# Gate of the first expert layer: first maximum worked in the PSUM bank of the logits, running sums left to TensorE, ranks issued three parts sooner

## The chip, the cores and the metric

One core of a Trainium2 chip runs the whole program. The metric is device time in microseconds (us), the median of the runs of a kernel. TensorE is written PE here, its weight loads PEld, VectorE DVE, ScalarE ACT, GpSimd POOL, SyncE SP.

## The reference

An attention with squared ReLU scores gives 9984 rows of 256 numbers. Two expert layers follow, each with 8 experts and one expert per row: a gate picks the expert by the first maximum of 8 logits, and the softmax weight of that maximum scales the expert's output.

```
x  = attention(u, v, z).reshape(9984, 256)
# first expert layer, for rows with x @ w_skip > 0, the others pass
e  = argmax(x @ w_gate);  p = softmax(x @ w_gate)[e]
x  = x + p * (relu(x @ w1[e]) @ w2[e])
# second expert layer, all rows
l  = x @ w_gate2 + modality_bias[modality_id]
e  = argmax(l);  p = softmax(l)[e]
out = p * (relu(x @ w1'[e]) @ w2'[e])
```

## The kernel before

The attention comes first; it sorts its rows by expert into a list in DRAM (`rows1`). The first expert layer (class `Moe1`) then walks that list in tiles of 348 rows (`P1` x `G1` = 116 x 3), one expert per tile, and the second layer (`Moe2`) walks `rows2` in tiles of 512. Everything is in the order in which the code is written: each engine runs its own instructions in that order, and waits where an operand is not ready or a buffer not free.

A tile is one call of `Moe.turn`. It has sixteen parts. In the parts h0 to h7 `hidden(f)` makes 128 of the 1024 hidden columns: six matmuls into a PSUM buffer `ph` (there are three), then a ReLU copy `hh` on ACT (L795) and the remainder `hl` on DVE (L796). In o0 to o7 `out_part(f)` multiplies `hh` and `hl` by the second weight, six matmuls again (L894). Between parts stand hooks, listed in `Moe1.PLAN`. The hook `("after",)` advances by one step the generator `Moe1.after`, which finishes the tile before: it forms that tile's logits for the second gate, picks the expert, ranks the rows within each expert, and sends them to `rows2`. So the gate of one tile is worked between the matmuls of the next.

Of its eleven steps these matter here, with the part behind which each stands: `logits` (h4) transposes the logits to rows on PE into a buffer `m` (pool `ps_m`, two buffers of one PSUM bank each, taken in turn) and DVE adds the bias (L939, tile `mlg`); `first` (h5) is `FirstMax`, five DVE instructions that mark the first maximum of three times 8 logits; `sums` (h6) masks the marks (L959, tile `ohbb`) and adds them up over the three groups (L963, `cumb`); `exp` (h7) is the exponential on ACT (L124); `rows(0)` (o0) and `rows(2)` (o1) transpose the output on PE into two more buffers `m` (L926) and write `x_out` on DVE (L930); `ranks` (o2) counts by three matmuls into a buffer `m` (L969 to L971) and makes the target indices on DVE (L974 to L980, L727). After the tile `send` scatters `x_out` to `rows2` from POOL, which also splits the second weight (L678) during h2 to o0.

There are 16 calls of `after`. Fifteen follow this order (`gate_first`). The last, under the first tile of the second layer, does the rows first, and its tile takes both buffers `m` for its own output (`take_y`) right behind `first` and `exp`.

Of the kernel before, what the change touches and what calls it, by code (L numbers as in the profile page):

```python
# [10 lines left out]
F32 = mybir.dt.float32  # L11
F32R = mybir.dt.float32r
BF16 = mybir.dt.bfloat16
I32 = mybir.dt.int32
AF = mybir.ActivationFunctionType
ALU = mybir.AluOpType
AX = mybir.AxisListType
# [6 lines left out]
E, F = 8, 1024  # L24
# [80 lines left out]
class FirstMax:  # L105


    def __init__(self, nc, pool, k, lg, P, n, tag):
        self.nc = nc
        sh = [P, n, E]  # L110
        t = lambda name, *sh: pool.tile([128, *sh], F32, name=name + tag)[:P]
        mx, self.df, self.hot = t("mx", n), t("df", n, E), t("hot", n, E)
        self.ex, self.sm = t("ex", n, E), t("sm", n)
        df, hot = self.df, self.hot
        nc.vector.tensor_reduce(mx, lg, axis=AX.X, op=ALU.max)
        nc.vector.tensor_tensor(df, lg, mx.unsqueeze(2).to_broadcast(sh), op=ALU.subtract)
        nc.vector.scalar_tensor_tensor(
            hot, df, 0.0, k.desc[:P].unsqueeze(1).to_broadcast(sh), op0=ALU.is_equal, op1=ALU.mult
        )
        nc.vector.tensor_reduce(mx, hot, axis=AX.X, op=ALU.max)  # L120
        nc.vector.tensor_tensor(hot, hot, mx.unsqueeze(2).to_broadcast(sh), op=ALU.is_equal)
# [622 lines left out]
class Moe:  # L744
# [74 lines left out]
    def turn(self, follow, after, hooks=None):  # L819

        nc, sh = self.nc, self.sh
        nxt = []

        def hook(what, *args):
            if what == "next":
                nxt.extend(follow())
                nxt[0].load_rows(nxt[2])
                sh.load(0, nxt[1])
            elif what == "after":
                next(after, None)  # L830
            elif what == "w2":
                sh.split(1, args[0], nc.gpsimd)
            elif what == "w1":
                sh.split(0, args[0], nc.vector)
            elif what == "x":
                nxt[0].x_transposed(args[0])
            elif what == "load w2":
                sh.load(1, nxt[1])
            else:
                what()  # L840

        plan = self.PLAN if hooks is None else hooks
        for h in plan["start"]:
            hook(*h)
        self.work({at: [lambda h=h: hook(*h) for h in hs] for at, hs in plan.items()})
        for _ in after:
            pass


class Moe1(Moe):  # L850
# [45 lines left out]
    def after(self, lim, current, ps=None, gate_first=True):  # L896

        nc, k, P, G, T = self.nc, self.k, self.P, self.G, self.T
        s, sh = self.p, self.sh
        y = s.tile([128, 2, T], F32, name="yS")  # L900
        yh = s.tile([128, 2, T], F32R, name="yh")
        yl = s.tile([128, 2, T], F32R, name="yl")
        x, xo, lt = self.x_cur, self.x_out[:P], self.lt
        lg = s.tile([128, G, E], F32, name="mlg")[:P]
        gate = {}

        def taken():
            for d in range(2):
                nc.scalar.copy(y[:, d], self.y[d])
                nc.scalar.copy(yh[:, d], self.y[d])  # L910

        def low(d):
            nc.vector.tensor_tensor(yl[:, d], y[:, d], yh[:, d].bitcast(F32), op=ALU.subtract)

        def logits_t():
            lt_ps = sh.ps_m.tile([2 * E, T], F32, name="m")
            for i, (d, m) in enumerate(((0, yh), (1, yh), (0, yl), (1, yl))):
                nc.tensor.matmul(lt_ps, self.wg[:, d], m[:, d], start=(i == 0), stop=(i == 3))
            nc.scalar.copy(lt[:2 * E], lt_ps)

        def rows(g0):
            y_ps = sh.ps_m.tile([128, 2, D], F32, name="m")[:P]
            gs = range(g0, min(g0 + 2, G))
            for g in gs:
                for d in range(2):
                    nc.tensor.transpose(  # L926
                        y_ps[:, g - g0, d * 128:(d + 1) * 128], y[:, d, g * P:(g + 1) * P], k.ident
                    )
            for g in gs:
                nc.vector.scalar_tensor_tensor(  # L930
                    xo[:, g, 0:D], y_ps[:, g - g0], x[:, g, C_G1:C_G1 + 1], x[:, g, 0:D], op0=ALU.mult, op1=ALU.add
                )

        def logits():
            lg_ps = sh.ps_m.tile([128, G, E], F32, name="m")[:P]
            for g in range(G):
                nc.tensor.matmul(lg_ps[:, g], lt[:, g * P:(g + 1) * P], k.pairs, start=True, stop=True)
            for g in range(G):
                nc.vector.scalar_tensor_tensor(  # L939
                    lg[:, g], lg_ps[:, g], x[:, g, C_G1:C_G1 + 1], x[:, g, C_B2:C_B2 + E],  # L940
                    op0=ALU.mult, op1=ALU.add,
                )

        def masks():
            gate["drop"] = s.tile([128, G], F32, name="mk_drop")[:P]
            nc.vector.memset(gate["drop"], 0.0)
            nc.vector.tensor_copy(sh.lim, lim.rearrange("p t o -> p (t o)"))
            mk = gate["mk"] = self.counted(sh.lim)[:, 0]
            nc.vector.tensor_scalar(gate["drop"], mk, -BIG, BIG, op0=ALU.mult, op1=ALU.add)
            gate["cum"] = s.tile([128, G + 1, E], BF16, name="cumb")[:P]  # L950
            nc.vector.memset(gate["cum"][:, 0], 0.0)

        def first():
            gate["first"] = FirstMax(nc, s, k, lg, P, G, "b")

        def sums():
            ohb, cum = s.tile([128, G, E], BF16, name="ohbb")[:P], gate["cum"]
            gate["ohb"] = ohb
            nc.vector.tensor_tensor(  # L959
                ohb, gate["first"].hot, gate["mk"].unsqueeze(2).to_broadcast([P, G, E]), op=ALU.mult  # L960
            )
            for g in range(G):
                nc.vector.tensor_tensor(cum[:, g + 1], cum[:, g], ohb[:, g], op=ALU.add)  # L963

        def ranks():
            w, ohb, cum = G * E, gate["ohb"], gate["cum"]
            flat = lambda t: t.rearrange("p n e -> p (n e)")
            rk_ps = (ps or sh.ps_m).tile([128, w + E], F32, name="m")
            nc.tensor.matmul(rk_ps[:P, 0:w], k.tri[:P, :P], flat(ohb), start=True, stop=False)  # L969
            nc.tensor.matmul(rk_ps[:P, 0:w], k.ones[:P, :P], flat(cum[:, 0:G]), start=False, stop=True)  # L970
            nc.tensor.matmul(rk_ps[:, w:], k.ones[:P], cum[:, G], start=True, stop=True)  # L971
            rk = s.tile([128, G, E], F32, name="rkb")[:P]
            carry = self.carry
            nc.vector.tensor_tensor(  # L974
                rk, rk_ps[:P, 0:w].rearrange("p (n e) -> p n e", n=G), carry[:P].to_broadcast([P, G, E]), op=ALU.add
            )
            nc.vector.tensor_tensor(carry[:, 0], carry[:, 0], rk_ps[:, w:], op=ALU.add)
            nc.vector.tensor_tensor(rk, rk, ohb, op=ALU.mult)
            at = s.tile([128, G], F32, name="atb")[:P]
            nc.vector.tensor_reduce(at, rk, axis=AX.X, op=ALU.add)  # L980
            self.sc.index(at, gate["drop"])

        def close():
            nc.vector.tensor_copy(xo[:, :, C_TID], x[:, :, C_TID])
            nc.vector.reciprocal(xo[:, :, C_G2], gate["first"].total())
            if current is not None:
                self.load_rows(current(), self.x_cur)

        both = lambda *f: lambda: [i() for i in f]
        exp = lambda: gate["first"].exp()  # L990
        begin = [both(masks, taken), lambda: low(0), lambda: low(1), logits_t]
        if gate_first:
            steps = begin + [logits, first, sums, exp, lambda: rows(0), both(lambda: rows(2), close), ranks]
        else:
            steps = begin + [lambda: rows(0), lambda: rows(2), logits, both(first, exp), both(close, sums), ranks]
        for step in steps[:-1]:
            step()
            yield
        steps[-1]()
# [319 lines left out]
```

## Time and profile before

| | before |
|---|---|
| median of 3 runs | 1509.66 us (1508.88 to 1510.91) |
| profiled execution | 1509.91 us |
| its span, first to last instruction | 1507.8 us |
| PE busy | 1471.7 us, 98% |
| DVE busy | 1082.8 us, 72% |
| ACT busy | 949.7 us, 63% |
| POOL busy | 614.7 us, 41% |

The span is what the trace covers; 2.1 us of the profiled execution lie around it. A busy PE means that matmuls follow one another; the duration of one in a row is longer than its distance to the next, since they overlap, so the distance of starts is what a matmul costs.

### The profile page before, as it was taken

The numbers are of one execution on the slowest core, as the hardware profiler recorded it, in microseconds if no ns is written. First come the engines' busy times: TensorE is split into PE (matmuls) and PEld (weight loads), VectorE is DVE, ScalarE is ACT, GpSimd is POOL, SyncE is SP. The second block draws the span as 40 slices with busy tenths as digits, with TensorE's granted clock in tenths as the row PEclk, the third lists the DMA queues.
The fourth block names the chain that finished last, engine by engine and source line by source line (L and its number), as shares of the span: only waits on it lengthen the run. The fifth ranks groups of instructions, "written<-read, shape, count | busy, mean of one in ns | idle before, by whom it ended". The sixth has DMA issues, their size and how long they took to land. (4 is left out here: it accounts for less than half of the span.)

```text
span 1507.8 us, 35395 instructions
## 1 busy us (share of the span) xinstructions
PE 1471.7 (98%) x11020; PEld 1268.7 (84%) x11020; DVE 1082.8 (72%) x2587; ACT 949.7 (63%) x1713; POOL 614.7 (41%) x865
## 2 busy tenths in 40 slices
PE   7999999999999999999999999999999999999998
PEld 5888888888887888888799999998888888888886
DVE  7788887888878888778787777777655555455553
ACT  7777777778777777776555555555445445455453
POOL 3022222223333233332365656655455354354454
PEclk9999999999999999999999999999999999999999
DMA  9011211112111141002145555554344433433440
GB/s 370 23 44 64 71 37 42 43 57 72 38 43 44 57 144 35 29 16 89 54 137 165 182 178 174 170 168 154 133 148 144 143 125 130 155 131 126 143 147 27
DMA packets 50212, 160.28 MB, mean 106 GB/s; under 512 B 13797, under 2 KB 15707, under 8 KB 40896
## 3 DMA queue, kind: packets, MB, share of 16 engines
q1 hardware_dynamic: 29232, 124.24, 25.1%
q0 software_dynamic: 20736, 34.71, 6.5%
q8 instruction: 61, 1.00, 0.3%
q14 instruction: 39, 0.32, 0.1%
q10 hardware_dynamic: 144, 0.02, 0.0%
HBM read 124.24 MB, written 46.55 MB: 113 GB/s over the span
## 5 line engine op out<-in xcount | busy, mean ns | idle before, releaser
L700 POOL DMA_INDIRECT rows<-r,ix x160 | 205.5, 1285 | 339.0 <-DVE xs L347 244.5
L334 PE MATMUL o<-ah,vh 64*128 64x512 f32 (+1 forms) x1560 | 311.4, 386 | 9.2 <-DVE xs L347 9.2
L334 PE MATMUL o<-al,vh 64*128 64x512 f32 (+1 forms) x1560 | 303.0, 384 | 0.0
L334 PE MATMUL o<-ah,vl 64*128 64x512 f32 (+1 forms) x1560 | 301.7, 383 | 0.0
L796 DVE SCALAR_TENSOR_TENSOR hl<-ph,hh 128x512 fp32r<-128x512 f32 (+1 forms) x288 | 176.5, 614 | 156.7 <-ACT hh L795 156.0
L678 POOL TENSOR_TENSOR w<-w2raw,w 128x256 fp32r<-128x256 f32 x282 | 198.8, 744 | 171.5 <-issue 154.8
L291 ACT ACTIVATE t<-s 128x1024 f32<-128x1024 f32 (+2 forms) x201 | 201.0, 1001 | 87.2 <-PE s L288 80.7
L305 DVE TENSOR_TENSOR al<-t,ah 128x1024 fp32r<-128x1024 f32 (+2 forms) x201 | 240.0, 1194 | 18.3 <-PE m L371 0.5
L795 ACT ACTIVATE hh<-ph 128x512 fp32r<-128x512 f32 (+1 forms) x288 | 155.8, 541 | 115.1 <-PE ph L793 102.9
L303 ACT ACTIVATE t<-t 128x1024 f32<-128x1024 f32 (+2 forms) x201 | 208.1, 1036 | 5.9
L793 PE MATMUL ph<-mxh,zA 128*128 128x512 f32 (+1 forms) x576 | 209.7, 364 | 2.1 <-PEq L1315 1.4
L304 DVE CAST ah<-t 128x1024 fp32r<-128x1024 f32 (+2 forms) x201 | 136.3, 678 | 103.1 <-ACT t L303 100.5
L793 PE MATMUL ph<-mxh,zB 128*128 128x512 f32 (+1 forms) x576 | 206.9, 359 | 1.0 <-issue 1.0
L793 PE MATMUL ph<-mxl,zA 128*128 128x512 f32 (+1 forms) x576 | 207.1, 360 | 0.3 <-DVE mxl L783 0.3
L334 PEld LDWEIGHTS o<-ah,vh 64*128 64x128 f32 x1560 | 150.5, 185 | 45.4 <-DVE xs L347 16.7
L334 PEld LDWEIGHTS o<-al,vh 64*128 64x128 f32 x1560 | 150.4, 185 | 27.3
L334 PEld LDWEIGHTS o<-ah,vl 64*128 64x128 f32 x1560 | 146.8, 185 | 27.4
L782 ACT CAST mxh<-m 128x512 fp32r<-128x512 f32 (+1 forms) x72 | 37.8, 526 | 167.2 <-PE m L778 163.3
L894 PE MATMUL o<-hh,w 128*128 128x348 f32 x512 | 129.5, 336 | 0.0
L793 PEld LDWEIGHTS ph<-mxh,zA 128*128 128x128 f32 x576 | 108.4, 188 | 19.6 <-issue 3.7
L288 PE MATMUL s<-zA,zB 64*128 64x512 f32 (+1 forms) x400 | 124.5, 389 | 0.0
L288 PE MATMUL s<-zB,zA 64*128 64x512 f32 (+1 forms) x400 | 122.1, 389 | 0.0
(236 smaller groups left out, 3050.8 us busy)
## 6 DMA issues: line engine op xcount, KB each, us to landing
w1raw<-in_w SPq DMA_DIRECT2D x36, 1024.0 KB, 6.8
w2raw<-in_w SPq DMA_DIRECT2D x36, 1024.0 KB, 5.1
x_in<-rows SPq DMA_DIRECT2D x20, 520.0 KB, 3.4
vraw<-in_v SPq DMA_DIRECT2D x20, 512.0 KB, 5.0
ut<-in_uT SPq DMA_DIRECT2D x20, 512.0 KB, 4.2
x_cur<-rows SPq DMA_DIRECT2D x16, 351.8 KB, 3.1
x_in<-rows SPq DMA_DIRECT2D x15, 351.8 KB, 3.2
rows<-x_in POOLq DMA_DIRECT2D x8, 536.0 KB, 12.0
```

The lines of the kernel that those rows point to most:

```text
L288: nc.tensor.matmul(s[:, i, :n], w[p, k], x[p, q], start=(j == 0), stop=(j == 2))
L291: nc.scalar.activation(t[:, i, :n], s[:, i, :n], AF.Relu, scale=SCALE)
L303: nc.scalar.activation(t[:, i, :n], t[:, i, :n], AF.Square)
L304: nc.vector.tensor_copy(h[:, i, :n], t[:, i, :n])
L305: nc.vector.tensor_tensor(l[:, i, :n], t[:, i, :n], h[:, i, :n].bitcast(F32), op=ALU.subtract)
L334: nc.tensor.matmul(o[half][d][:, :n], w[p, d * 128:d * 128 + 128], x[p, :n], start=(u == 0 and j == at[0]), stop=(u == 9 and j == at[-1]),)
L678: lo_engine.tensor_tensor(l[:, c], src[:, c], h[:, c].bitcast(F32), op=ALU.subtract)
L700: i = tc.nc.gpsimd.indirect_dma_start(out=out, out_offset=bass.IndirectOffsetOnAxis(ap=ix, axis=0), in_=rows, in_offset=None, bounds_check ...
L793: nc.tensor.matmul(ps, w, x, start=(i == 0), stop=(i == len(mms) - 1))
L795: nc.scalar.activation(h, ps, AF.Relu)
L796: nc.vector.scalar_tensor_tensor(l, ps, 0.0, h.bitcast(F32), op0=ALU.max, op1=ALU.subtract)
L894: nc.tensor.matmul(self.y[d], w[:, dd], h[f], start=(f == 0 and i == 0), stop=(f == 7 and i == 2))
```

## The change

`FirstMax` may now be given the tiles for the difference and the marks. In `Moe1.after` the buffer `m` of the logits is four times as wide: the transposed logits, the logits with bias, the difference and the marks are four pieces of one PSUM bank. The masking stands in `first`; the step `sums` and its running sums are gone, and `ranks` adds with matmuls by ones instead, six matmuls in place of three. `exp` is now behind h6, `ranks` behind h7, and the last DVE instruction of the old `ranks` stays behind o2 as `place`.

```diff
@@ -105,11 +105,12 @@
 class FirstMax:
 
 
-    def __init__(self, nc, pool, k, lg, P, n, tag):
+    def __init__(self, nc, pool, k, lg, P, n, tag, df=None, hot=None):
         self.nc = nc
         sh = [P, n, E]
         t = lambda name, *sh: pool.tile([128, *sh], F32, name=name + tag)[:P]
-        mx, self.df, self.hot = t("mx", n), t("df", n, E), t("hot", n, E)
+        mx = t("mx", n)
+        self.df, self.hot = (t("df", n, E), t("hot", n, E)) if df is None else (df, hot)
         self.ex, self.sm = t("ex", n, E), t("sm", n)
         df, hot = self.df, self.hot
         nc.vector.tensor_reduce(mx, lg, axis=AX.X, op=ALU.max)
@@ -901,7 +902,6 @@
         yh = s.tile([128, 2, T], F32R, name="yh")
         yl = s.tile([128, 2, T], F32R, name="yl")
         x, xo, lt = self.x_cur, self.x_out[:P], self.lt
-        lg = s.tile([128, G, E], F32, name="mlg")[:P]
         gate = {}
 
         def taken():
@@ -932,7 +932,8 @@
                 )
 
         def logits():
-            lg_ps = sh.ps_m.tile([128, G, E], F32, name="m")[:P]
+            gate["ps"] = sh.ps_m.tile([128, 4, G, E], F32, name="m")[:P]
+            lg_ps, lg = gate["ps"][:, 0], gate["ps"][:, 1]
             for g in range(G):
                 nc.tensor.matmul(lg_ps[:, g], lt[:, g * P:(g + 1) * P], k.pairs, start=True, stop=True)
             for g in range(G):
@@ -947,28 +948,26 @@
             nc.vector.tensor_copy(sh.lim, lim.rearrange("p t o -> p (t o)"))
             mk = gate["mk"] = self.counted(sh.lim)[:, 0]
             nc.vector.tensor_scalar(gate["drop"], mk, -BIG, BIG, op0=ALU.mult, op1=ALU.add)
-            gate["cum"] = s.tile([128, G + 1, E], BF16, name="cumb")[:P]
-            nc.vector.memset(gate["cum"][:, 0], 0.0)
 
         def first():
-            gate["first"] = FirstMax(nc, s, k, lg, P, G, "b")
-
-        def sums():
-            ohb, cum = s.tile([128, G, E], BF16, name="ohbb")[:P], gate["cum"]
-            gate["ohb"] = ohb
+            ps = gate["ps"]
+            gate["first"] = FirstMax(nc, s, k, ps[:, 1], P, G, "b", ps[:, 2], ps[:, 3])
+            gate["ohb"] = s.tile([128, G, E], BF16, name="ohbb")[:P]
             nc.vector.tensor_tensor(
-                ohb, gate["first"].hot, gate["mk"].unsqueeze(2).to_broadcast([P, G, E]), op=ALU.mult
+                gate["ohb"], gate["first"].hot, gate["mk"].unsqueeze(2).to_broadcast([P, G, E]), op=ALU.mult
             )
-            for g in range(G):
-                nc.vector.tensor_tensor(cum[:, g + 1], cum[:, g], ohb[:, g], op=ALU.add)
 
         def ranks():
-            w, ohb, cum = G * E, gate["ohb"], gate["cum"]
+            w, ohb = G * E, gate["ohb"]
             flat = lambda t: t.rearrange("p n e -> p (n e)")
             rk_ps = (ps or sh.ps_m).tile([128, w + E], F32, name="m")
             nc.tensor.matmul(rk_ps[:P, 0:w], k.tri[:P, :P], flat(ohb), start=True, stop=False)
-            nc.tensor.matmul(rk_ps[:P, 0:w], k.ones[:P, :P], flat(cum[:, 0:G]), start=False, stop=True)
-            nc.tensor.matmul(rk_ps[:, w:], k.ones[:P], cum[:, G], start=True, stop=True)
+            for g in range(1, G):
+                nc.tensor.matmul(
+                    rk_ps[:P, g * E:w], k.ones[:P, :P], flat(ohb[:, 0:G - g]), start=False, stop=(g == G - 1)
+                )
+            for g in range(G):
+                nc.tensor.matmul(rk_ps[:, w:], k.ones[:P], ohb[:, g], start=(g == 0), stop=(g == G - 1))
             rk = s.tile([128, G, E], F32, name="rkb")[:P]
             carry = self.carry
             nc.vector.tensor_tensor(
@@ -976,9 +975,11 @@
             )
             nc.vector.tensor_tensor(carry[:, 0], carry[:, 0], rk_ps[:, w:], op=ALU.add)
             nc.vector.tensor_tensor(rk, rk, ohb, op=ALU.mult)
-            at = s.tile([128, G], F32, name="atb")[:P]
-            nc.vector.tensor_reduce(at, rk, axis=AX.X, op=ALU.add)
-            self.sc.index(at, gate["drop"])
+            gate["at"] = s.tile([128, G], F32, name="atb")[:P]
+            nc.vector.tensor_reduce(gate["at"], rk, axis=AX.X, op=ALU.add)
+
+        def place():
+            self.sc.index(gate["at"], gate["drop"])
 
         def close():
             nc.vector.tensor_copy(xo[:, :, C_TID], x[:, :, C_TID])
@@ -990,9 +991,9 @@
         exp = lambda: gate["first"].exp()
         begin = [both(masks, taken), lambda: low(0), lambda: low(1), logits_t]
         if gate_first:
-            steps = begin + [logits, first, sums, exp, lambda: rows(0), both(lambda: rows(2), close), ranks]
+            steps = begin + [logits, first, exp, ranks, lambda: rows(0), both(lambda: rows(2), close), place]
         else:
-            steps = begin + [lambda: rows(0), lambda: rows(2), logits, both(first, exp), both(close, sums), ranks]
+            steps = begin + [lambda: rows(0), lambda: rows(2), logits, both(first, exp), close, both(ranks, place)]
         for step in steps[:-1]:
             step()
             yield
```

In the built program this moves the following rows. The names are the program's: `ph`, `hh`, `hl`, `o` and `m` as above, `w` the second weight, `tri` and `ones` constants. First PE, in a tile of the first layer outside the loop (the loop's tile has the same rows with register instructions between). Before, the end of h7 and o0:

```order
L793 MATMUL ph<-mxh,zA_113 128x348
L793 MATMUL ph<-mxl,zA_113 128x348
L793 MATMUL ph<-mxh,zB_114 128x348
L894 MATMUL o_11060<-hh_11037,w_11033 128x348 x2
L894 MATMUL o_11060<-hl_11045,w_11033 128x348
L894 MATMUL o_11061<-hh_11037,w_11033 128x348 x2
L894 MATMUL o_11061<-hl_11045,w_11033 128x348
L926 MATMUL m<-ident,yS 116x128 x4
```

And now the same place:

```order
L794 MATMUL ph<-mxl,zA_113 128x348
L794 MATMUL ph<-mxh,zB_114 128x348
L964 LDWEIGHTS tri
L964 MATMUL m<-ohbb,tri 116x24
L966 LDWEIGHTS ones
L966 MATMUL m<-ohbb,ones 116x16
L966 LDWEIGHTS ones
L966 MATMUL m<-ohbb,ones 116x8
L970 LDWEIGHTS ones
L970 MATMUL m<-ohbb,ones 128x8
L970 LDWEIGHTS ones
L970 MATMUL m<-ohbb,ones 128x8
```

A third such pair and then o0 (L895) follow. The matmuls on the masked marks `ohbb` stood behind o2 as three, and now stand between h7 and o0 as six.

DVE in the last tile of the first layer, from the logits on. Before:

```order
L939 SCALAR_TENSOR_TENSOR mlg<-m,x_cur 116x8 x3
L796 SCALAR_TENSOR_TENSOR hl_11050<-ph,hh_11042 128x348
L115 TENSOR_REDUCE mxb<-mlg 116x3
L116 TENSOR_TENSOR dfb<-mlg,mxb 116x24
L117 SCALAR_TENSOR_TENSOR hotb<-dfb,desc 116x24
L120 TENSOR_REDUCE mxb<-hotb 116x3
L121 TENSOR_TENSOR hotb<-hotb,mxb 116x24
L796 SCALAR_TENSOR_TENSOR hl_11051<-ph,hh_11043 128x348
L959 TENSOR_TENSOR ohbb<-hotb,mk 116x24
L963 TENSOR_TENSOR cumb<-cumb,ohbb 116x8 x3
L796 SCALAR_TENSOR_TENSOR hl_11052<-ph,hh_11044 128x348
```

And now:

```order
L940 SCALAR_TENSOR_TENSOR m<-m,x_cur 116x8 x3
L797 SCALAR_TENSOR_TENSOR hl_11050<-ph,hh_11042 128x348
L116 TENSOR_REDUCE mxb<-m 116x3
L117 TENSOR_TENSOR m<-m,mxb 116x24
L118 SCALAR_TENSOR_TENSOR m<-m,desc 116x24
L121 TENSOR_REDUCE mxb<-m 116x3
L122 TENSOR_TENSOR m<-m,mxb 116x24
L956 TENSOR_TENSOR ohbb<-m,mk 116x24
L797 SCALAR_TENSOR_TENSOR hl_11051<-ph,hh_11043 128x348
L797 SCALAR_TENSOR_TENSOR hl_11052<-ph,hh_11044 128x348
L973 TENSOR_TENSOR rkb<-m,carry 116x24
L976 TENSOR_TENSOR carry<-carry,m 128x8
```

The masking stands one `hl` sooner, the running sums are gone, the additions on the ranks follow the last `hl`, and the logits, difference and marks lie in `m`.

PE in the last call of `after`, under the first tile of the second layer, with what each row waits for (the number behind an engine's name only marks its semaphore). Before, o0 begins:

```order
L1056 MATMUL o_11060<-w_11033,hh_11037 128x512 [waits Pool_49]
L1059 MATMUL o_11060<-w_11033,hl_11045 128x256
L1056 MATMUL o_11061<-w_11033,hh_11037 128x512
L1059 MATMUL o_11061<-w_11033,hl_11045 128x256
L1056 MATMUL m<-w_11033,hh_11037 128x512 [waits DVE_49]
L1059 MATMUL m<-w_11033,hl_11045 128x256
L1056 MATMUL m<-w_11033,hh_11037 128x512 [waits DVE_49]
```

And now:

```order
L1057 MATMUL o_11060<-w_11033,hh_11037 128x512 [waits Pool_49]
L1060 MATMUL o_11060<-w_11033,hl_11045 128x256
L1057 MATMUL o_11061<-w_11033,hh_11037 128x512
L1060 MATMUL o_11061<-w_11033,hl_11045 128x256
L1057 MATMUL m<-w_11033,hh_11037 128x512 [waits DVE_49]
L1060 MATMUL m<-w_11033,hl_11045 128x256
L1057 MATMUL m<-w_11033,hh_11037 128x512 [waits Activation_49]
```

The order is the same; the second matmul into a buffer `m`, the one that held the logits, waits for ACT in place of DVE.

## Rows read from the trace of the kernel before

**Rows 1.** One loop tile: stretch, length, PE, PEld, DVE, ACT, POOL busy, PEclk, DMA, GB/s.

```profile
925.92:943.87 17.95, 17.95 (x122) 17.58 (x122) 14.14 (x47) 10.65 (x25) 11.19 (x18) 1.00 0.55 178
```

**Rows 2.** Waits of PE, 759 to 1063 us (waiter, releaser, us, times, longest).

```profile
PE m L969 <- DVE x_out L930: 3.8, 4, 1.6
```

**Rows 3.** Timeline of that tile, DVE: the chain behind h5 (start, us, instruction).

```profile
933.79 0.52 DVE L796 SCALAR_TENSOR_TENSOR hl<-ph,hh 128x348 fp32r<-128x348 f32 x1 [0.72 <-ACT hh L795]
934.23 0.17 DVE L115 TENSOR_REDUCE mxb<-mlg 116x3 f32<-116x24 f32 x1
...
934.64 0.63 DVE L117 SCALAR_TENSOR_TENSOR hotb<-dfb,desc 116x24 f32<-116x24 f32 x1
...
935.52 0.45 DVE L121 TENSOR_TENSOR hotb<-hotb,mxb 116x24 f32<-116x24 f32 x1
...
936.33 0.17 DVE L959 TENSOR_TENSOR ohbb<-hotb,mk 116x24 bf16<-116x24 f32 x1
```

**Rows 4.** Timeline of that tile, PE: o0, row transposes, ranks.

```profile
934.78 0.48 PE L894 MATMUL o<-hh,w 128*128 128x348 f32 x2
...
935.74 0.60 PE L926 MATMUL m<-ident,yS 128*116 128x128 f32 x4
...
937.45 0.38 PE L926 MATMUL m<-ident,yS 128*116 128x128 f32 x2
...
938.61 0.18 PE L969 MATMUL m<-ohbb,tri 116*116 116x24 bf16 x1
938.64 0.20 PE L970 MATMUL m<-cumb,ones 116*116 116x24 bf16 x1
938.69 0.17 PE L971 MATMUL m<-cumb,ones 116*128 116x8 bf16 x1
938.72 0.41 PE L894 MATMUL o<-hh,w 128*128 128x348 f32 x1
```

**Rows 5.** Timeline of the third tile, POOL, DVE and PE: the longest of the four waits.

```profile
803.89 4.89 POOL L678 TENSOR_TENSOR w<-w2raw,w 128x256 fp32r<-128x256 f32 x7
...
805.82 2.31 DVE L116 TENSOR_TENSOR dfb<-mlg,mxb 116x24 f32<-116x24 f32 x1
...
809.86 0.32 PE L894 MATMUL o<-hl,w 128*128 128x348 f32 x1
...
810.89 0.86 DVE L930 SCALAR_TENSOR_TENSOR x_out<-m,x_cur 116x256 f32<-116x256 f32 x2
...
811.81 0.22 PE L969 MATMUL m<-ohbb,tri 116*116 116x24 bf16 x1 [1.62 <-DVE x_out L930]
811.88 0.20 PE L970 MATMUL m<-cumb,ones 116*116 116x24 bf16 x1
```

**Rows 6.** Small DVE instructions by line (ns minimum, median, maximum; 16 tiles).

```profile
L939 DVE SCALAR_TENSOR_TENSOR mlg<-m,x_cur x48: 216/218/220, 766.0 to 1049.4; 116x8 f32<-116x8 f32 x48
...
L974 DVE TENSOR_TENSOR rkb<-m,carry x16: 174/176/177, 775.1 to 1056.3; 116x24 f32<-116x24 f32 x16
...
L978 DVE TENSOR_TENSOR rkb<-rkb,ohbb x16: 175/177/178, 775.3 to 1056.6; 116x24 f32<-116x24 f32 x16
...
L121 DVE TENSOR_TENSOR hotb<-hotb,mxb x16: 182/450/757, 768.4 to 1052.8; 116x24 f32<-116x24 f32 x16
```

**Rows 7.** Timeline of the first tile, DVE and PE: the chain undisturbed, and o0.

```profile
767.59 0.17 DVE L115 TENSOR_REDUCE mxb<-mlg 116x3 f32<-116x24 f32 x1
...
768.23 0.18 DVE L120 TENSOR_REDUCE mxb<-hotb 116x3 f32<-116x24 f32 x1
...
768.30 0.48 PE L894 MATMUL o<-hh,w 128*128 128x348 f32 x2
```

**Rows 8.** Timeline of the last call of `after`, PE, DVE, ACT.

```profile
1050.72 0.39 PE L1056 MATMUL m<-w,hh 128*128 128x512 f32 x1
...
1051.12 0.17 DVE L115 TENSOR_REDUCE mxb<-mlg 116x3 f32<-116x24 f32 x1
...
1051.93 0.22 ACT L124 ACTIVATE exb<-dfb 116x24 f32<-116x24 f32 x1 [0.94 <-DVE dfb L116]
```

## The prediction

> **What bounds the kernel now.** I read the share of busy time first, then the waits of PE, then one tile of the first expert layer in order of time. In a tile of the loop PE is busy for 17.95 of 17.95 us at a PEclk of 1.00, while DVE is busy for 14.14, ACT for 10.65 and POOL for 11.19 [rows 1]. So in this stage a microsecond more or less of matmuls or of waiting on PE is a microsecond of the program, and work taken off DVE is worth nothing by itself. The list of waits says where PE does stand still: in the stage of the first layer only the ranks wait for another engine, four times in fifteen tiles, 3.8 us in all [rows 2]. The reader should keep two things apart here: what the four waits cost, which the change can give back at most once, and what a new wait in every tile would cost.
>
> The four waits come from the chain of small DVE instructions behind the logits. In the third tile the difference (L116) took 2.31 us while POOL ran its split of the second weight; everything behind it on DVE slid, `x_out` was done at 811.75 (810.89 + 0.86), and the ranks' first matmul, due 0.16 us behind the matmul at 809.86, began at 811.81 [rows 5]. That is 1.79 us late, of which the trace books 1.62 as idle, and 0.06 us after the instruction it waited for. An undelayed L121 takes 182 ns, its median is 450 and its longest 757, while instructions with an operand in PSUM, such as L974, stay between 174 and 177 in all sixteen tiles [rows 6].
>
> **The change part by part.** *The chain without delays.* With logits, difference and marks in PSUM, each of the five instructions and the masking has at most one tensor operand in SBUF, like L974. So I cost the chain as it runs undisturbed: from L115 to L120 in the first tile three steps take 0.64 us, 0.213 each [rows 7]. Five steps and the masking's own 0.17 [rows 3] make 1.24 us from L115's start to finished marks. Reading PSUM costs nothing extra by rows of like size: L974, with its input in PSUM, has a median of 176 ns, L978, all in SBUF, 177 [rows 6]. No row shows DVE writing to PSUM; I take the same price, and as the upper bound that of the dearest small instruction with a PSUM input, L939 at 218 ns for 8 columns [rows 6], 0.04 us more for each of six, 0.24 us in a tile. Below, steps half as long would be 0.5 us less in a tile, but no row has dependent steps as close as that.
>
> [...]
>
> *The ranks' new place.* The matmuls on the marks move from behind o2 to between h7 and o0. In the tile of rows 3 and 4, PE gets there at 934.78, when o0 began before [rows 4]. The marks cannot be ready then: `hl` of h5, which stands ahead of the chain on DVE and waits for ACT's `hh`, starts at 933.79, and the chain's first instruction at 934.23 [rows 3]. Nothing in the change starts that sooner, for it hangs on PE's own h5. So the marks are done at 934.23 + 1.24 = 935.47, PE hears of it 0.06 us later [rows 5], and it has stood for 935.53 - 934.78 = 0.75 us. Behind the waiting matmul stands all of o0 and the rest of the tile, and rows 1 leave no idle time in which it could be made up. Twelve of the fifteen tiles look like this one; in the first two and the last the chain starts earlier against o0, as in the first tile, where the wait comes to 767.59 + 1.30 - 768.30 = 0.59 us [rows 7]. Together 12 x 0.75 + 3 x 0.59 = **10.8 us more**; the upper bound of the write price adds 15 x 0.24 = 3.6.
>
> *Six matmuls for three.* Before, the three stand 0.03 and 0.05 us apart, and o0's successor 0.03 behind [rows 4]. Each added one brings its own load of weights; I take 0.05, with 0.03 as the lower bound: 3 x 0.05 x 16 = **2.4 us more** (1.4 at the least). After a wait the second of them followed 0.07 us behind the first, not 0.03 [rows 5]: 15 x 0.04 = **0.6 more**.
>
> *The old waits.* The chain no longer meets POOL, and the ranks no longer need a buffer that `x_out` must free: the four waits go. At 3.8 us of idle time [rows 2] and, by rows 5, 0.17 + 0.04 us each that are not booked as idle, **4.6 us less**.
>
> *The exponential and the buffers.* The buffer of the logits is now held until DVE has masked the marks and ACT has read the difference. In the ordinary tile `rows(0)` is the next to use it, at 935.74 before [rows 4]; with PE 0.75 us and six matmuls later it comes near 936.75, while the exponential, even if it waits for the masking, is done at 935.47 + 0.06 + 0.22 = 935.75, its length as in [rows 8]: covered by 1.0 us. `rows(2)` needs the ranks' buffer, which DVE reads behind the last `hl`, itself now behind the exponential on ACT: `hh` of h7 by 936.2, `hl` by 936.8, the two additions by 937.2; PE wants the buffer at 937.45 + 1.0 [rows 4]: covered by over 1 us. If that cover were gone it would cost the excess in each tile.
>
> In the last call of `after` there is no such cover. There the second layer's first tile takes the buffer for its own output in o0, and the order shows that this matmul now waits for ACT, not for DVE, though DVE still reads the marks there: so the exponential must itself come behind the masking. The matmul ran at 1050.72; the chain starts at 1051.12 [rows 8]. 1051.12 + 1.24 + 0.06 + 0.22 + 0.06 = 1052.70: **2.0 us more**, once.
>
> *Free.* Three additions and a memset in a tile leave DVE; it has 3.8 us to spare in a tile [rows 1], and what waits there now is PE. The index is made at the same place (`place`, behind o2), and its touch on POOL, the scatters and every load keep their places, so no DMA moves. The clock was 1.00 throughout the tile [rows 1] and I leave it there.
>
> **Sum.** +10.8 + 2.4 + 0.6 + 2.0 - 4.6 = +11.2 us. The profiled execution took 1509.91 us, 2.1 outside its span of 1507.8; 1509.9 + 11.2 = 1521.1. The median of the runs is 0.25 us lower, less than they differ among themselves. I say 1521 us, 0.7% slower.
>
> **Rivals.** *Writes to PSUM are dear.* At L939's price the program comes to 1521.1 + 3.6 + 0.2 = 1525; at twice that surcharge, to 1529. Against it: the pair L974 and L978. [...] Chance 0.14.
>
> *The chain is still delayed by POOL.* Then it runs as in rows 3: L121 ends at 935.97, the marks near 936.2, and PE waits 1.46 us, 0.71 more than I say; four tiles would have the long block of rows 5, about 2.1 more. 11 x 0.71 + 4 x 2.1 = 16: 1537. For it: one operand (the constant of L117, the maxima) is still in SBUF. Against it: L974 and L939 have one as well, and never vary [rows 6]. Chance 0.04.
>
> *The marks are there in time: not slower.* If the instructions overlapped, so that the chain took no more than 934.78 - 0.06 - 934.23 = 0.49 us, PE would never stand at the ranks, the last call's wait would be 1.2, and the program would take 1509.9 - 4.6 + 2.4 + 1.2 = 1508.9. For it: three L939 in a row need no result of each other and pass quickly. Against it: each step of the chain reads the one before, and needed 0.21 [rows 7]. Up to a wait of 0.2 us in a tile, a chain of 0.7, it would stay within the bound given below. Chance 0.06, with another 0.03 that the extra matmuls and the last wait vanish as well and it ends at 1505.
>
> *In between*, a chain of 0.9 to 1.0 us: 1515 to 1518. Chance 0.06.
>
> **How the numbers follow.** My own case has the remaining 0.67, from 1518 (extra matmuls at 0.03, steps of 0.2 us) to 1524. From 1516 to 1528 lie that case, the dear writes for the most part and half of what is in between: 0.8 and a little. A measurement of this kernel tells some 0.2%, 3 us, from no change. Faster by more 0.03, within it 0.06, slower 0.91.
>
> **What would show it.** The list of waits: PE at the ranks (L964) for DVE's masking (L956), fifteen times, 0.6 to 0.75 us each; one of about 2 us at the second `m` in the last call, for the exponential; the four on `x_out` gone. The timeline: the chain's instructions at 170 to 190 ns, none longer, 0.21 apart, and the exponential behind L956. Tiles of the loop 0.9 us longer than 17.95. I am wrong if the ranks follow h7 without a gap, if the steps are much closer than 0.2 us, or if the loop's tiles keep their length.

## The result, and the profile after

The changed kernel takes 1521.82 us (median of 5 runs, 1521.69 to 1523.01) against 1509.66 us before: a ratio of 1.0077, 95% interval 1.0067 to 1.0088. It is slower by 12.2 us; 11.2 were forecast, with a range of 1516 to 1528.

The page of the changed kernel, its first part:

```profile
span 1519.8 us, 35342 instructions
PE 1474.6 (97%) x11068; PEld 1273.2 (84%) x11068; DVE 1067.4 (70%) x2523; ACT 945.8 (62%) x1713; POOL 606.4 (40%) x865
```

DVE has 15.4 us less to do than before and PE 2.9 us more, and the span is 12.0 us longer: the time did not go into work. Nor did it go into TensorE's clock: the mean granted clock is 0.997 in the profile of before and 0.998 in this one. The same busy times for one tile of the loop (columns as in [rows 1]):

```profile
930.84:949.69 18.85, 18.25 (x127) 17.74 (x125) 13.63 (x43) 10.73 (x25) 10.95 (x18) 1.00 0.53 164
```

The tile is 0.90 us longer than the one of before, and 0.60 us of it PE stands idle. The waits of PE in the first layer's stage say for whom:

```profile
PE m L964 <- DVE ohbb L956: 8.6, 15, 0.6
PE ph L794 <- issue: 2.4, 1, 2.4
PE m L1057 <- ACT exb L125: 1.8, 1, 1.8
```

Where [rows 2] had four waits on `x_out`, there are fifteen on the masked marks `ohbb`, one in each tile with `gate_first`, and one on the exponential in the last call. The wait marked "issue" stands behind the loop and is taken up at the end.

The tile in order of time, DVE; this answers to [rows 3]:

```profile
938.73 0.52 DVE L797 SCALAR_TENSOR_TENSOR hl<-ph,hh 128x348 fp32r<-128x348 f32 x1 [0.46 <-ACT hh L796]
939.16 0.17 DVE L116 TENSOR_REDUCE mxb<-m 116x3 f32<-116x24 f32 x1
939.37 0.19 DVE L117 TENSOR_TENSOR m<-m,mxb 116x24 f32<-116x24 f32 x1
939.60 0.19 DVE L118 SCALAR_TENSOR_TENSOR m<-m,desc 116x24 f32<-116x24 f32 x1
939.82 0.18 DVE L121 TENSOR_REDUCE mxb<-m 116x3 f32<-116x24 f32 x1
940.04 0.19 DVE L122 TENSOR_TENSOR m<-m,mxb 116x24 f32<-116x24 f32 x1
940.26 0.18 DVE L956 TENSOR_TENSOR ohbb<-m,mk 116x24 bf16<-116x24 f32 x1
...
941.73 0.17 DVE L973 TENSOR_TENSOR rkb<-m,carry 116x24 f32<-116x24 f32 x1
941.94 0.16 DVE L976 TENSOR_TENSOR carry<-carry,m 128x8 f32<-128x8 f32 x1
```

And PE and ACT in the same tile, which answers to [rows 4]:

```profile
939.58 0.32 PE L794 MATMUL ph<-mxh,zB 128*128 128x348 f32 x1
940.50 0.17 PE L964 MATMUL m<-ohbb,tri 116*116 116x24 bf16 x1 [0.60 <-DVE ohbb L956]
940.52 0.25 PE L966 MATMUL m<-ohbb,ones 116*116 116x16 bf16 x2
940.63 0.22 PE L970 MATMUL m<-ohbb,ones 116*128 116x8 bf16 x3
940.71 0.56 PE L895 MATMUL o<-hh,w 128*128 128x348 f32 x2
...
941.74 0.60 PE L926 MATMUL m<-ident,yS 128*116 128x128 f32 x4
...
943.44 0.38 PE L926 MATMUL m<-ident,yS 128*116 128x128 f32 x2
...
940.56 0.19 ACT L125 ACTIVATE exb<-m 116x24 f32<-116x24 f32 x1 [0.96 <-DVE ohbb L956]
```

The chain is clean: six instructions 0.21 to 0.23 us apart, none delayed. The marks are done at 940.44. The last matmul of h7 began at 939.58, so the ranks could have begun at 939.74; they begin at 940.50, 0.76 us late. The exponential also waits for the masking, as inferred from the order, and both buffers are free in time: the transposes at 941.74 and 943.44 follow without a gap.

The last call of `after`, PE, DVE and ACT, which answers to [rows 8]:

```profile
1061.43 0.28 PE L1060 MATMUL m<-w,hl 128*128 128x256 f32 x1
1063.50 0.50 PE L1057 MATMUL m<-w,hh 128*128 128x512 f32 x1 [1.79 <-ACT exb L125]
...
1061.94 0.17 DVE L116 TENSOR_REDUCE mxb<-m 116x3 f32<-116x24 f32 x1
...
1063.05 0.18 DVE L956 TENSOR_TENSOR ohbb<-m,mk 116x24 bf16<-116x24 f32 x1
...
1063.26 0.19 ACT L125 ACTIVATE exb<-m 116x24 f32<-116x24 f32 x1 [1.45 <-DVE ohbb L956]
```

PE's second `m` waits for the exponential, that for the masking, and that for a chain which starts only when PE is already there.

### The profile page after: what moved, and what is told of

It is laid out like the page before. It is cut to its first block, busy times and chain, and to the rows that moved or that the text cites. A ratio compares the mean times of both kernels' runs of the same rounds, so it can differ in the third digit from the quotient of the medians.

```text
span 1519.8 us, 35342 instructions
## 1 busy us (share of the span) xinstructions
PE 1474.6 (97%) x11068; PEld 1273.2 (84%) x11068; DVE 1067.4 (70%) x2523; ACT 945.8 (62%) x1713; POOL 606.4 (40%) x865
## 3 DMA queue, kind: packets, MB, share of 16 engines
q1 hardware_dynamic: 29232, 124.24, 25.1%
## 5 line engine op out<-in xcount | busy, mean ns | idle before, releaser
L701 POOL DMA_INDIRECT rows<-r,ix x160 | 198.3, 1239 | 333.4 <-DVE xs L348 239.4
L895 PE MATMUL o<-hh,w 128*128 128x348 f32 x512 | 129.3, 335 | 0.0
```

The costliest lines, as they stand in the source:

```text
L701: i = tc.nc.gpsimd.indirect_dma_start(out=out, out_offset=bass.IndirectOffsetOnAxis(ap=ix, axis=0), in_=rows, in_offset=None, bounds_check ...
L895: nc.tensor.matmul(self.y[d], w[:, dd], h[f], start=(f == 0 and i == 0), stop=(f == 7 and i == 2))
```

## The experiments

The theory: PE stands between h7 and o0 because the chain on DVE, which begins behind `hl` of h5, ends 0.76 us after PE gets there; PSUM helps the chain, and the added matmuls cost little. The first rival: the price lies in small DVE work through PSUM, or in six matmuls instead of three. The second: the place between h7 and o0 costs by itself. Seven runs tell them apart. Each ratio is to runs of the kernel before on the same chip, whose medians were 1509.58 us for the first four and 1510.38 us for the last three. It is not the ratio of the two medians, which can differ from it by 0.001.

### The ranks back behind o2

```diff
-steps = begin + [logits, first, exp, ranks, lambda: rows(0), both(lambda: rows(2), close), place]
+steps = begin + [logits, first, exp, lambda: None, lambda: rows(0), both(lambda: rows(2), close), both(ranks, place)]
```

> The changed kernel with the ranks' matmuls and DVE work put back behind o2; first maximum in PSUM and six matmuls stay. Theory (PE stands between h7 and o0 for the marks): the fifteen waits of about 0.76 us go, 11 us; the old four waits stay away, since the chain still does not meet POOL; the wait of 2 us in the last call stays. 1509.9 - 4.6 + 1.6 + 2.0 = 1509 us, loop tiles of about 18.05 us. Rival (the price is that of small DVE work through PSUM or of three more matmuls): 1518 or more.

Measured: 1508.76 us, ratio 1.0000 (0.9991 to 1.0010). Its waits of PE in the first layer's stage:

```profile
PE ph L794 <- issue: 2.0, 1, 2.0
PE m L1057 <- ACT exb L125: 1.8, 1, 1.8
```

Neither the fifteen waits nor the old four are there; loop tiles take 18.06 us. With PSUM and all six matmuls kept, the place of the ranks alone takes back the whole loss. So neither the six matmuls nor DVE work through PSUM make the loss by themselves. Whether such work is slow while PE waits for it can't be seen here, where PE does not wait; for that stand the rows above, 0.17 to 0.19 us for each instruction of the chain, and the run back in SBUF below. With these the first rival is out.

### The chain one part sooner

```diff
-steps = begin + [logits, first, exp, ranks, ...
+steps = begin + [both(logits, first), exp, lambda: None, ranks, ...
```

> The changed kernel with the first maximum and the masking one part sooner, behind h4 together with the logits; the ranks stay between h7 and o0. Theory: the wait is set by hl of h5, which stands ahead of the chain on DVE. Without it the marks are done some 0.4 us before PE gets to the ranks, and the fifteen waits go though the place is the same: 1509 us. hl of h5 comes over 1 us later, but no matmul of the h parts needs it. Rival (the place between h7 and o0 costs by itself, or the delayed hl holds up PE): 1515 to 1521.

Measured: 1510.29 us, ratio 1.0007 (0.9998 to 1.0016). Its timeline in one tile, DVE and PE:

```profile
927.92 0.77 DVE L940 SCALAR_TENSOR_TENSOR m<-m,x_cur 116x8 f32<-116x8 f32 x3
928.72 0.18 DVE L116 TENSOR_REDUCE mxb<-m 116x3 f32<-116x24 f32 x1
...
929.83 0.18 DVE L956 TENSOR_TENSOR ohbb<-m,mk 116x24 bf16<-116x24 f32 x1
930.01 0.52 DVE L797 SCALAR_TENSOR_TENSOR hl<-ph,hh 128x348 fp32r<-128x348 f32 x1
...
930.00 0.32 PE L794 MATMUL ph<-mxh,zB 128*128 128x348 f32 x1
930.16 0.18 PE L964 MATMUL m<-ohbb,tri 116*116 116x24 bf16 x1
```

The ranks stand where the change put them and follow h7 after 0.16 us, the distance at which the matmuls of h7 follow one another: the marks were done at 930.01, 0.15 us before PE came. Loop tiles take 18.11 us, 0.05 more than with the ranks behind o2. So neither the place nor the late `hl` costs more than that, and the second rival is out: the wait is a matter of what stands ahead of the chain on DVE.

A margin of 0.4 us had been expected. The missing quarter lies in the three additions of the bias, which the chain now follows at once. In the kernel before, which writes the logits to SBUF, they took less:

```profile
932.58 0.48 DVE L939 SCALAR_TENSOR_TENSOR mlg<-m,x_cur 116x8 f32<-116x8 f32 x3
```

None of the three needs another's result. Their starts are 0.13 us apart where they write to SBUF, and 0.26 to 0.27 where they write to the PSUM bank that they read; in the run with the chain back in SBUF, the next one, the three take 0.48 us again.

### The chain back in SBUF

```diff
+        mlg = s.tile([128, G, E], F32, name="mlg")[:P]
...
-            lg_ps, lg = gate["ps"][:, 0], gate["ps"][:, 1]
+            lg_ps, lg = gate["ps"][:, 0], mlg
...
-            gate["first"] = FirstMax(nc, s, k, ps[:, 1], P, G, "b", ps[:, 2], ps[:, 3])
+            gate["first"] = FirstMax(nc, s, k, mlg, P, G, "b")
```

> The changed kernel with the logits, the difference and the marks back in SBUF; order, six matmuls and the ranks' place stay. Theory: in PSUM the chain is free of POOL; back in SBUF it is delayed by POOL again, and since the ranks now wait for it each delay falls on PE: 0.7 us more in eleven tiles, about 2.1 more in four, 2.0 less in the last call, whose buffer is free again: 1521.8 + 16 - 2 = 1536 us. Rival (PSUM makes no difference to the chain): 1520 us.

Measured: 1532.92 us, ratio 1.0162 (1.0149 to 1.0175). One tile of it in order of time, POOL, DVE and PE:

```profile
943.33 4.93 POOL L679 TENSOR_TENSOR w<-w2raw,w 128x256 fp32r<-128x256 f32 x7
...
946.75 0.18 DVE L117 TENSOR_TENSOR dfb<-mlg,mxb 116x24 f32<-116x24 f32 x1
946.97 0.64 DVE L118 SCALAR_TENSOR_TENSOR hotb<-dfb,desc 116x24 f32<-116x24 f32 x1
947.65 0.18 DVE L121 TENSOR_REDUCE mxb<-hotb 116x3 f32<-116x24 f32 x1
947.86 0.43 DVE L122 TENSOR_TENSOR hotb<-hotb,mxb 116x24 f32<-116x24 f32 x1
948.33 0.18 DVE L956 TENSOR_TENSOR ohbb<-hotb,mk 116x24 bf16<-116x24 f32 x1
...
948.57 0.17 PE L964 MATMUL m<-ohbb,tri 116*116 116x24 bf16 x1 [1.28 <-DVE ohbb L956]
```

Its list of waits has, at the ranks:

```profile
PE m L964 <- DVE ohbb L956: 21.0, 15, 3.1
```

While POOL splits the weight, two of the instructions with two tensor inputs in SBUF, L118 and L122, take 0.64 and 0.43 us in place of 0.18; the reduction between them, with one, keeps its 0.18. L122 ends at 948.29, 0.03 us behind the last instruction of POOL's split (948.26), and the masking, which also has two such inputs but starts behind that, takes 0.18. L117, the third of them in the chain, was not delayed in this tile. That it is the split that delays L118 and L122 is inferred from these times; why it spares L117 was not shown. PSUM was worth 11 us to this order of work (12.4 us of waiting at the ranks, less the 1.8 of the last call, whose wait is not in this list): each delay of the chain, which the order of before mostly hid, falls on PE once the ranks wait for it. My 1536 was 3 us too high, for it had four long blocks as in [rows 5], and here only one wait is that long, 3.1 us. The rival, that PSUM makes no difference to the chain, is out.

### The running sums by matmuls alone

```diff
 # the kernel before, ranks behind o2
-            for g in range(G):
-                nc.vector.tensor_tensor(cum[:, g + 1], cum[:, g], ohb[:, g], op=ALU.add)
...
-            nc.tensor.matmul(rk_ps[:P, 0:w], k.ones[:P, :P], flat(cum[:, 0:G]), start=False, stop=True)
-            nc.tensor.matmul(rk_ps[:, w:], k.ones[:P], cum[:, G], start=True, stop=True)
+            for g in range(1, G):
+                nc.tensor.matmul(rk_ps[:P, g * E:w], k.ones[:P, :P], flat(ohb[:, 0:G - g]), start=False, stop=(g == G - 1))
+            for g in range(G):
+                nc.tensor.matmul(rk_ps[:, w:], k.ones[:P], ohb[:, g], start=(g == 0), stop=(g == G - 1))
```

> The kernel before with one part of the change alone: the running sums made by six matmuls behind o2 in place of three DVE additions and three matmuls. Theory: each added matmul costs 0.03 us, 1.6 us in all, and the four old waits shrink by the additions, 0.5 us each: 1509.5 us. Rival (0.05 to 0.07 each, as I took before): 1512 us.

Measured: 1507.27 us, ratio 0.9990 (0.9981 to 1.0000), loop tiles of 18.06 us. One of the four old waits is left:

```profile
PE m L965 <- DVE x_out L930: 1.0, 1, 1.0
```

The matmuls cost 0.11 us in a tile, and a DVE relieved of three additions reaches `x_out` sooner, so that 2.8 of the 3.8 us of old waits go, which pays for them. The rival, 1512 us, is out.

### The last call back in SBUF

As the run with the ranks behind o2, and only the call without `gate_first` keeps logits, difference and marks in SBUF:

```diff
...
-            lg_ps, lg = gate["ps"][:, 0], gate["ps"][:, 1]
+            lg_ps, lg = gate["ps"][:, 0], gate["ps"][:, 1] if gate_first else mlg
...
+            tiles = (ps[:, 2], ps[:, 3]) if gate_first else ()
+            gate["first"] = FirstMax(nc, s, k, gate["lg"], P, G, "b", *tiles)
```

> As the run with the ranks back behind o2, and in the last call of after alone the logits, difference and marks in SBUF. Theory: the wait of 1.8 us at the second m in the last call goes, since the buffer is free once the logits are read; the rest stays: 1507 us, with tiles of 18.06 in the loop. Rival (PE waits there for something else): the 1.8 us stay, 1509 us.

Measured: 1506.78 us, ratio 0.9975 (0.9966 to 0.9984). The wait on the exponential is gone from its list of waits: the buffer caused it. This kernel is faster than the one before (by 0.25%) and than the changed one.

### PSUM for the chain and nothing else

```diff
...
 # on top of the one above: running sums on DVE behind h7, three matmuls behind o2
-steps = begin + [logits, first, exp, lambda: None, lambda: rows(0), ...
+steps = begin + [logits, first, exp, sums, lambda: rows(0), ...
```

> As the run before it in this list, with the running sums again as three additions on DVE (behind h7) and three matmuls behind o2: of the whole change only the first maximum in PSUM and the earlier masking are left, and those not in the last call. Theory: loop tiles of 17.95 again, no wait at the ranks, no wait in the last call: 4.6 us less than before, 1505 us. Rival (the old four waits come back with the sums on DVE): 1507 to 1509 us.

Measured: 1506.64 us, ratio 0.9972 (0.9961 to 0.9983). The busy times of one of its loop tiles (columns as in [rows 1]):

```profile
913.00:930.95 17.95, 17.95 (x123) 17.58 (x122) 14.07 (x46) 10.72 (x24) 11.02 (x18) 1.00 0.56 179
```

Its list of waits has, at the ranks:

```profile
PE m L974 <- DVE x_out L931: 0.6, 1, 0.6
```

The tile is that of before, and three of the four old waits are gone: 3.7 us by the medians, 2.6 to 5.9 by the interval, against an expected 4.6. The exponential, too, still stands one part sooner than before. This kernel and the one above cannot be told apart.

### The ranks two parts sooner, not three

```diff
-steps = begin + [logits, first, exp, ranks, lambda: rows(0), both(lambda: rows(2), close), place]
+steps = begin + [logits, first, exp, lambda: rows(0), ranks, both(lambda: rows(2), close), place]
```

> The changed kernel with the ranks' matmuls one part later, behind o0, and the row transposes of rows(0) in their place behind h7. Theory: o0 and four transposes, 1.4 us, lie between h7 and the ranks, more than the 0.76 us that the marks are late, so the fifteen waits go while the ranks are still two parts sooner than before: 1509 us, loop tiles of 18.06. Rival (ranks that come sooner cost anywhere, or the logits' buffer, which the ranks now take, is not yet free): 1512 or more.

Measured: 1510.95 us, ratio 1.0003 (0.9994 to 1.0012). One tile, DVE and PE:

```profile
933.99 0.18 DVE L956 TENSOR_TENSOR ohbb<-m,mk 116x24 bf16<-116x24 f32 x1
...
935.46 0.87 DVE L930 SCALAR_TENSOR_TENSOR x_out<-m,x_cur 116x256 f32<-116x256 f32 x2
...
934.84 0.18 PE L964 MATMUL m<-ohbb,tri 116*116 116x24 bf16 x1
...
936.48 0.40 PE L926 MATMUL m<-ident,yS 128*116 128x128 f32 x2
```

No wait at the ranks: the marks were done at 934.17 and the ranks ran at 934.84. Loop tiles take 18.14 to 18.19 us, 0.1 more than with the ranks behind o2. That tenth stands ahead of the transposes of `rows(2)` (L926), which begin 0.26 to 0.29 us behind the matmul before them in place of 0.16. In twelve tiles they begin 0.15 us behind the end of `x_out` of `rows(0)` (936.33 here): with the ranks in this place the buffer `m` that they take is the one that this `x_out` reads. That `x_out` is what they wait for is inferred from the order and the constant distance. Sooner ranks bring nothing here, and by the buffers they cost about 1.5 us, half of what the rival asks.

## Why the prediction was right

Its mechanism is the one the runs show, and its sum holds in every term but the ranks' matmuls. *The new wait*: forecast 10.8 us, 0.75 in an ordinary tile and 0.59 in three; measured 11.0 over the fifteen, 0.76 and 0.63. *The chain*: forecast 1.24 us from L116's start, measured 1.28 (939.16 to 940.44). *The last call*: forecast 2.0, measured 1.95 (2.07 between the two starts, less the 0.12 they lie apart elsewhere). *The old waits*: forecast to go, and gone.

*The ranks' matmuls* were the term that I mis-sized: 3.0 us with the slow start after a wait, measured 1.6. From the first of the six to o0 it takes 0.21 us, against 0.11 for the three, and no slow start shows (0.02 in place of 0.07). The load of `tri` ran at 939.58 here, ahead of the wait; in the tile of [rows 5] it ran at 811.80, behind it. The list by line, changed kernel, shows a difference that I had not used:

```profile
L966 PEld LDWEIGHTS <-ones x32: 128/130/133, 770.1 to 1068.8; 116*116 116x116 bf16 x32
L970 PEld LDWEIGHTS <-ones x48: 95/96/123, 770.2 to 1069.0; 116*128 116x128 bf16 x48
```

Loads of 116 columns take 130 ns and their matmuls follow 0.053 us apart; loads of 128 columns take 96 ns (123 for the first of each three) and theirs follow 0.025 apart, and three of the six are of that kind. Why the wider loads are the faster ones was not shown.

The terms as measured make 11.0 + 1.6 + 1.95 - 4.6 = 10.0, and the span grew by 12.0. Of the rest, 1.2 us lie ahead of the first layer's stage (its second tile starts at 760.44, before at 759.27), where the two programs are alike, 1.3 in the wait marked "issue" (2.37 against 1.05), and some 0.5 in the tiles, which are 0.90 us longer in the loop where the terms give 0.86. The second layer's next two tiles give back 1.0 (47.76 us before, 46.74 now), for which no term stands. The first two vary from run to run, below. That the forecast of 11.2 came nearer to 12.0 than the terms do is luck: what it had too much for the matmuls stands in for time that it did not foresee.

The rivals. *Writes to PSUM are dear*: an instruction of the chain takes 4 to 9 ns more than undelayed in SBUF (191 against 182 for the three that write to PSUM), not the 40 of the nearest row; the chain's 0.04 us over the forecast is about their sum. *POOL* did not delay the chain. *The marks* were not there in time; where an experiment had them there in time, behind o2, sooner on DVE or behind o0, the program came out at 1508.8 to 1511.0 us, near the 1508.9 of that rival.

One remark of the prediction is too strong: that work taken off DVE is worth nothing by itself. In the tiles where PE waits for DVE it shortens the wait, by 2.8 us in the run of the running sums.

## What to carry to other kernels

On an engine that never idles, an instruction moved forward must be set against the end of the chain that feeds it, counted from where the chain can start on its own engine, with what stands ahead of it there. Part of a change may be good and its placing undo it: the first maximum in PSUM with the earlier masking was worth some 4 us (2.6 to 5.9), and the three parts by which the ranks moved cost 11 us of waiting. And a buffer that is held for longer has to be followed to its next user in every variant of the schedule: the one call with another order paid 2 us.

## What the runs showed of the hardware

The chain of small DVE instructions, each reading the one before, cost nearly the same from PSUM to PSUM as in SBUF: its three instructions that write 116x24 fp32 to PSUM took 190 to 192 ns each in all sixteen tiles of the changed kernel, against an undelayed 182 in SBUF. In the tile shown above they took that while POOL split the weight (935.23 to 940.88). Beside the split two of the three, L118 and L122, took 0.64 and 0.43 us in SBUF, in the tile of the run with the chain back there; in the kernel before, the three have medians of 184, 629 and 450 ns and maxima of 2306, 664 and 757. For small instructions that do not need each other's results it was otherwise: the three additions of the bias start 0.26 to 0.27 us apart when they write to the PSUM bank that they read, and 0.13 apart when they write to SBUF. In the changed kernel DVE stands idle behind them for 0.46 us, so this costs nothing there.

PE waits once behind the loop, inside h0 of the tile after it, with nothing that the profile names as its cause: 0.9 to 2.9 us in the nine profiles. In three of them (before, changed, and the chain one part sooner) the profile shows one packet on the queue q8, of the kind "instruction", in the 5 to 6 us around that wait; whether the wait comes from it was not tested.

The first layer's second tile began between 755.9 and 760.4 us in the same profiles, though the attention ahead of it is the same program. Much of that goes with TensorE's clock. The busy times from 735 to 765 us, columns as in [rows 1], for the kernel before and for the run with the chain one part sooner:

```profile
735.00:765.00 30.00, 27.20 (x174) 25.02 (x172) 25.13 (x90) 16.71 (x48) 15.17 (x20) 0.89 0.28 96
735.00:765.00 30.00, 26.28 (x183) 23.60 (x181) 25.17 (x94) 17.63 (x51) 16.25 (x22) 1.00 0.28 94
```

The granted clock of this stretch is 0.89 in three profiles (before, changed, ranks back behind o2), 0.94 in three (the last three experiments) and 1.00 in three. Within it, in the kernel before, the clock is 0.50 from 751 to 757 us and 1.00 up to 750 and from 758. The first layer's first tile takes 25.4, 24.8 to 25.1 and 22.6 us in the same three groups. PE had stood for 2.5 to 2.9 us in that tile in the first two groups and for 1.9 in the third, so not all of the difference is the clock's.

Behind the loop, from the last tile of the first layer to the end of the first tile of the second, the clock is 1.00 in four profiles, the two kernels compared here among them, 0.96 to 0.97 in three, and 0.90 in the runs with the ranks behind o2 and with the chain one part sooner. The spread of the runs goes with it: of the twelve with the ranks behind o2, six have a mean clock of 0.998 and take 1507.8 us on average, and two have 0.993 and take 1513.6. What lets the clock fall in one run and not in the next is open. Some 3 us of a single run, and at times 6, are therefore not the change's doing, and differences as small as those of the last four experiments need many runs.
